# A softmax-attention and S4-convolution kernel: zero matmuls ahead of the first projections, wide gate matmuls, U and H in half-size transfers, norms in pairs, a later set deadline, 71 VectorE sets

## The chip, the cores and the metric

One core of a Trainium2 chip. The metric is the device time of one execution in microseconds (us). The engines are TensorE (PE, with its weight loads shown as PEld), VectorE (DVE), ScalarE (ACT), GpSimd (POOL) and SyncE (SP), whose queue issues nearly all DMAs. Each engine runs its own instructions in their order and waits on semaphores for the others.

## The reference

```python
def reference(A_x, A_wqkv, A_wo, B_u, ..., gate_w):      # x: (1, 2048, 512), u is x
    x = A_x
    g = sigmoid((x * gate_w).sum(-1, keepdims=True))
    a = attention(x, wqkv, wo)          # 32 heads of 16, softmax over all 2048 keys
    b = s4(x, A, B, C, log_dt, Dskip)   # y = causal_conv(x, K) + x * Dskip, per channel
    return g * a + (1 - g) * b
# K[d, l] = Re sum_n C[d,n] exp(dt A[d,n] l) dt B[d,n], l < 2048, n < 128
```

Inputs and output are bf16; scores, sums and the convolution's accumulators are fp32.

## The kernel before

**Attention.** 32 blocks (8 head pairs times 4 stretches of 512 queries) of 16 key tiles are worked as 512 "quads" of four 128x512 score tiles: 2048 tiles in all, three to a group, 683 groups. For group g, `qk(g)` puts three score tiles on PE into one of two PSUM score banks (`SC0`, `SC1`), `ex(g)` takes their exponential on ACT into slots of the ring `ET` (`NS` = 15 slots of 512), and `pv` multiplies a quad with the values into the PSUM bank `OA`. Zero matmuls (`wm`, in `zero` and `qk`) fill PE where its work is thin.

**Sets.** Exponentials are the largest work of ACT, so `decide` gives some tiles to DVE: a set is 12 tiles in four consecutive groups, whose third tiles are computed on DVE (`bits`, four conversions to the bits of a power of two, then `batch`: two masks and a product, into `DZ` and `DU`). In these groups ACT has 128x1024 in place of 128x1536. `WIN` lists the windows of groups in which sets are allowed, their buffers, the least distance and how much idle time DVE must have gathered. The last quad of a block (`kt == 15`, in `pvq`) waited until the set belonging to the block had been multiplied.

**Norms.** After a block, `norm_a` transposes `OA` out of PSUM, `norm_b` divides by the row sums (one reciprocal, one product), and for each second block `norm_c` transposes the pair into `OnT`.

**Convolution.** `bases`, `tables`, `zpart` and `kstage` build K on DVE and PE and write it to DRAM (`gm_kd`); `xrows` writes shifted copies of x (`gm_xs`). `ystage` multiplies: 32 double passes of four quarters, each quarter reading a Toeplitz block `H` (256 KB, five buffers) and a strip `U` (542 KB per double pass, two buffers), loaded by `yloads`. The result, times 1 - g, goes through `Yst` and DRAM into `Yl`.

**Gate and output.** `gate` computes x times gate_w as 64 matmuls with one moving column, then the sigmoid. `outs` multiplies the attention by Wo, and one DVE operation per 128 rows gives g times it plus `Yl`.

**The order.** Nothing is ordered at run time: a planner (`Sched`, `Prog`) with costs per operation (`c`), DMA landing (`lat`), DMA bandwidth (`b`, and `pace` for transfers that keep distance) and priorities writes one instruction order per engine when the kernel is built. A changed cost therefore moves instructions on all engines. The start is by hand: loads on ACT's and SP's queues, nine zero matmuls, transposes of x, then Q and K projections, and the first scores.

Of the kernel before, what the change touches and what calls it, by code (L numbers as in the profile page):

```python
# [304 lines left out]
class Sched:  # L305
# [140 lines left out]
def declare(nc, es):  # L446
# [20 lines left out]
    sb("OT", 512, FP32)  # L467
# [10 lines left out]
    sb("gwT", 4)  # L478
# [53 lines left out]
    B["gd"] = Buf("gd", "dr", P * 16, FP32)  # L532
    B["gd"].t = nc.dram_tensor("gm_gd", [P, 16], FP32)
# [94 lines left out]
def record(nc, p, B, ins):  # L628
# [177 lines left out]
    def seat():  # L806
        while 3 * len(held) + 3 <= len(tiles) or len(tiles) == NSL and len(held) < NG:
            g = len(held)
            n = 2 if g in vec else len(slots(g))
            if plan["at"] + n > NS:  # L810
                plan["at"] = 0
# [3 lines left out]
            plan["at"] = (held[g] + n) % NS  # L815

    def pvq(q, prev, wait):
# [3 lines left out]
        if kt == 15 and wait:  # L821
            yield ("AFTER", wait)
# [7 lines left out]
        sch.open(b if kt < 15 else None)  # L830

# [37 lines left out]

    def ex(g):  # L870
# [3 lines left out]
        op("ACT", lambda a: a.activation(ET(512 * e, [[1, 512 * n]]), sc(0, [[1, 512 * n]]), AF.Exp, scale=DH ** -0.5),  # L874
           [(sc, i, g) for i in range(n)], [(ET, e + i, ts[i]) for i in range(n)] + [(B["tk"], g)], c=.055 + .4267 * n, lat=.105)
# [25 lines left out]
    def batch(i):  # L901
# [3 lines left out]
        def mask(t, a, o, W):  # L905
# [5 lines left out]
        yield ("DVE", dv(2048, 2))  # L911
        op("DVE", lambda v: v.tensor_tensor(u(0, [[1, 2048]]), z(0, [[1, 2048]]), u(0, [[1, 2048]]), ALU.mult),  # L912
           R + [(u, 0, ("m", i))], [(u, 0, i)], c=dv(2048, 2))
# [5 lines left out]
        for t in (u, z):  # L919
            yield ("PE", QUAD)  # L920
            for k, j in enumerate(sets[i]["js"]):
                pv_mm(4 * q + j, t, 512 * k, [(u, 0, i) if t is u else (z, k, (i, k, "t"))], QUAD if k == 0 else 0)
        sch.mark(f"dvp{i}")

    def norm_a(b):
        op("DVE", lambda v: v.transpose(OT(0, [[1, 512]]), OA(0, [[1, 512]])), [(OA, 0, b)], [(OT, 0, b)], c=.64)  # L926

    def norm_b(b):
        w = b % 2
        op("DVE", lambda v: v.reciprocal(Rz(16 * w, [[1, 16]]), OT(16, [[32, 16]])), [(OT, 0, b)], [(Rz, w)], c=.25)  # L930
        op("DVE", lambda v: v.tensor_tensor(ON(16 * w, [[32, 16], [1, 16]]), OT(0, [[32, 16], [1, 16]]),
                                            Rz(16 * w, [[1, 16], [0, 16]]), ALU.mult), [(OT, 0, b), (Rz, w)], [(ON, w)], c=.35)
# [183 lines left out]

    def tables():
        H5 = dv(512, 2)
        yield ("AFTER", "DL80")
# [44 lines left out]
    def kstage(blk):  # L1164
# [3 lines left out]
        Tm = B[f"T{blk % NT}"]  # L1168
# [41 lines left out]
    def xrows():  # L1210
# [8 lines left out]
        for q4 in range(4):  # L1219
            for s0 in range(0, T, 4):  # L1220
# [3 lines left out]
                    [(xP, (0, q4))] + [(xP, (1, s1)) for s1 in range(s0, s0 + 4)], [(xs, (q4, s0))], c=.7, lat=4, b=.86, pace=True)  # L1224
# [4 lines left out]
    UL = 8 * UW - R8 // 2  # L1229

    def yloads():
        yield ("AFTER", YGO)
        for v in range(2 * NBLK):
# [4 lines left out]
            for i in range(2):  # L1238
                yield ("SP", .7)
                dma("SP", lambda e, v=v, U=U, i=i: e.dma_start(U(UL * i, [[1, UL + i]]), xs.dram(v * 16 * UW + R8 - 1 + UL * i, [[D * UW, T], [-1, R8], [1, UL + i]])),  # L1240
                    [(xs, (v // 8, s0)) for s0 in range(0, T, 4)], [(U, i, v)], c=.7, lat=3.5, b=.72, pace=True)
            for q in range(4):
                u = 4 * v + q
                H = B[f"H{u % NHB}"]
                if u >= NHB:
                    yield ("AFTER", f"yh{u - NHB}")
                yield ("AFTER", f"kd{v // 2}")
                yield ("SP", .6)
                dma("SP", lambda e, u=u, H=H: e.dma_start(H(0, [[1, T * HW]]), kd.dram(u * HR * HW + (33 - T) * HW, [[HW, T], [T * HW, R8], [1, T * HW]])),
                    [(kd, (u // 8, u // 2 % 4))], [(H, 0, u)], c=.6, lat=3.5, b=.68, pace=True)  # L1250
# [336 lines left out]
```

## Time and profile before

| | us |
|---|---|
| median of 3 runs | 857.8 (856.04 to 859.12) |
| profiled execution, whole | 860.27 |
| its span | 858.2 |
| first exponential starts | 13.54 |
| last DVE transpose after the exponentials starts | 849.19 |
| mean granted TensorE clock | 0.952 |

A row of instruction groups reads: source line, engine, operation, output <- input with partitions x elements, count | busy us, mean ns of one | idle us just before, and what ended it. Source line L643 is the one line that issues every matmul, so groups are told apart by their tiles. A row of stretches reads: start:end, length, busy us (and count) of PE, PEld, DVE, ACT, POOL, then the granted PE clock (1.00 is full), the share of the DMA engines and GB/s. In the list of instructions in order of time, the first two numbers are start and duration, and the bracket is the idle time before it and its releaser.

### The profile page before, as it was taken

Reading aid. Unit: us, or ns where it says so; the run is one execution under the profiler, and the core shown is the slowest. Engines: PE = TensorE matmul, PEld = TensorE weight load, DVE = VectorE, ACT = ScalarE, POOL = GpSimd, SP = SyncE. Lnnn points to the kernel's source line nnn. Section 1 sums busy time; section 2 is a strip of 40 time slices with the busy share of each in tenths; the row PEclk is TensorE's granted clock in tenths of the full one; section 3 lists DMA queues with packets and bytes.
Section 4 is the critical chain, followed back from the end, with each engine's and each line's share of the span. In section 5 each row is a group of like instructions: output and inputs, shape, how many; then the busy total and the mean of one; then the engine's idle time right before and its main releaser. Section 6 shows DMA issues by size and latency. Waiting matters only on the chain.

```text
span 858.2 us, 35245 instructions
## 1 busy us (share of the span) xinstructions
PE 716.2 (83%) x16105; PEld 317.2 (37%) x16105; DVE 732.2 (85%) x1233; ACT 819.8 (96%) x692; POOL 10.0 (1%) x15
## 2 busy tenths in 40 slices
PE   7879878888887888798888878888887888889884
PEld 3232234342244444354444434444442443322221
DVE  6999896599988979877979786998969889989972
ACT  6999999999988999999999999999999999999895
POOL 4000000000000000000000000000000000000000
PEclk7996899999989999989999999999999999999988
DMA  9464002124576665555445665445566754100000
GB/s 202 81 105 45 12 1 43 26 44 157 152 179 154 162 190 144 142 129 128 111 126 141 177 160 151 98 116 144 119 175 109 204 153 118 19 27 27 28 1 26
DMA packets 154310, 92.71 MB, mean 108 GB/s; under 512 B 116017, under 2 KB 124594, under 8 KB 153778
## 3 DMA queue, kind: packets, MB, share of 16 engines
q1 hardware_dynamic: 152434, 89.55, 42.9%
q8 instruction: 126, 2.06, 1.0%
q10 hardware_dynamic: 1728, 0.92, 0.5%
q14 instruction: 22, 0.18, 0.1%
HBM read 64.46 MB, written 17.31 MB: 95 GB/s over the span
## 4 chain that ended last, share of the span: by engine, by line
ACT 75%; PE 15%; DVE 6%; issue 2%; DMA 1%; ACTq 0%; DVEq 0%
ACT ET L874 75%; PE SC L643 6%; PE MB L643 5%; PE OA L643 4%; DVE DZ L895 2%; DVE fo L1367 1%; DVE DU L912 1%; DMA Wq<-in_A_wqkv_dram 1%; DVE DU L906 0%; DVE Yst L1281 0%; DVE OT L926 0%; DVE DZ L906 0%; ACTq L647 0%; DVE OnT L936 0%; DVE Kt L1190 0%
## 5 line engine op out<-in xcount | busy, mean ns | idle before, releaser
L874 ACT ACTIVATE ET<-SC 128x1536 bf16<-128x1536 f32 (+1 forms) x683 | 813.0, 1460 | 24.3 <-PE SC L643 19.2
L643 PE MATMUL SC<-Qm,KT 32*128 32x512 bf16 x2048 | 288.8, 398 | 110.3 <-ACT ET L874 91.4
L895 DVE TENSOR_SCALAR DZ<-SC 128x512 uint16<-128x512 f32 x268 | 179.6, 685 | 44.0 <-PE SC L643 42.7
L643 PE MATMUL OA<-ET,VE 128*32 128x512 bf16 x1780 | 183.1, 403 | 2.3 <-issue 1.2
L643 PEld LDWEIGHTS SC<-Qm,KT 32*128 32x128 bf16 x2048 | 71.9, 91 | 284.7 <-ACT ET L874 229.2
L643 PE MATMUL OA<-wm 128*32 128x256 bf16 (+3 forms) x845 | 170.3, 364 | 1.2 <-DVE wm L695 1.2
L643 PE MATMUL MB<-U,H 128*16 128x96 bf16 (+15 forms) x8192 | 130.4, 200 | 9.4 <-issue 8.5
L643 PEld LDWEIGHTS MB<-U,H 128*16 128x16 bf16 x8192 | 115.2, 109 | 55.1 <-issue 37.2
L643 PEld LDWEIGHTS OA<-ET,VE 128*32 128x32 bf16 x1780 | 45.9, 94 | 105.1 <-issue 100.1
L912 DVE TENSOR_TENSOR DU<-DZ,DU 128x2048 bf16<-128x2048 bf16 x67 | 82.2, 1227 | 0.5
L940 DVE TENSOR_TENSOR T<-B,DL 128x512 bf16<-128x512 bf16 x192 | 68.8, 415 | 0.0
L643 PEld LDWEIGHTS MB<-T,Z 128*32 128x32 bf16 x2048 | 51.7, 177 | 10.3 <-issue 8.3
L643 PE MATMUL MB<-T,Z 128*32 128x64 bf16 (+1 forms) x2048 | 52.9, 246 | 1.5 <-issue 0.7
L643 PEld LDWEIGHTS OA<-wm 128*32 128x32 bf16 (+2 forms) x845 | 44.1, 97 | 10.4 <-issue 9.1
L906 DVE TENSOR_SCALAR DU<-DZ 128x2048 uint16<-128x2048 uint16 x67 | 46.3, 692 | 0.4
L906 DVE TENSOR_SCALAR DZ<-DZ 128x2048 uint16<-128x2048 uint16 x67 | 45.8, 684 | 0.3
L926 DVE STREAM_TRANSPOSE OT<-OA 128x512 f32<-128x512 f32 x32 | 22.9, 715 | 17.9 <-PE OA L643 17.4
L1281 DVE TENSOR_TENSOR Yst<-MB,gt 128x512 bf16<-128x512 f32 x32 | 21.9, 685 | 16.6 <-PE MB L643 16.3
L940 DVE TENSOR_TENSOR ft<-FP,L 128x1024 f32<-128x1024 f32 (+1 forms) x32 | 34.5, 1113 | 0.5
L643 PE MATMUL OA<-DZ,VE 128*32 128x512 bf16 x268 | 28.0, 402 | 1.9 <-issue 1.1
L643 PE MATMUL OA<-DU,VE 128*32 128x512 bf16 x268 | 27.7, 400 | 0.0
L1190 DVE STREAM_TRANSPOSE Kt<-MB 128x512 f32<-128x512 f32 x16 | 11.4, 712 | 14.5 <-PE MB L643 14.3
(123 smaller groups left out, 435.3 us busy)
## 6 DMA issues: line engine op xcount, KB each, us to landing
H<-gm_kd SPq DMA_DIRECT2D x128, 256.0 KB, 4.0
U<-gm_xs SPq DMA_DIRECT2D x32, 271.2 KB, 4.1
U<-gm_xs SPq DMA_DIRECT2D x32, 271.0 KB, 3.5
T<-B SPq DMA_DIRECT2D x32, 128.0 KB, 3.4
gm_bd<-B16s SPq DMA_DIRECT2D x3, 1024.0 KB, 4.7
B<-gm_bd SPq DMA_DIRECT2D x12, 256.0 KB, 4.0
gm_kd<-Ks SPq DMA_DIRECT2D x64, 40.0 KB, 3.1
gm_xs<-xP SPq DMA_DIRECT2D x16, 136.0 KB, 6.4
```

Source lines behind the costliest of these rows:

```text
L643: op("PE", lambda t: t.matmul(out(), lhsT(), rhs(), start=start, stop=stop, skip_group_check=True, **kw), R, W, c=c, lat=.15, a=a, cfg=cfg)
L874: op("ACT", lambda a: a.activation(ET(512 * e, [[1, 512 * n]]), sc(0, [[1, 512 * n]]), AF.Exp, scale=DH ** -0.5), [(sc, i, g) for i in ran ...
L895: op("DVE", lambda v: v.tensor_scalar(z.u16(512 * k, [[1, 512]]), sc(1024, [[1, 512]]), XS, XB, ALU.mult, ALU.add), [(sc, 2, g)], [(z, k, ...
L906: op("DVE", lambda v: v.tensor_scalar(t.u16(0, [[1, 2048]]), z.u16(0, [[1, 2048]]), a, o, ALU.bitwise_and, ALU.bitwise_or), R, W, c=.07 + ...
L912: op("DVE", lambda v: v.tensor_tensor(u(0, [[1, 2048]]), z(0, [[1, 2048]]), u(0, [[1, 2048]]), ALU.mult), R + [(u, 0, ("m", i))], [(u, 0, ...
L926: op("DVE", lambda v: v.transpose(OT(0, [[1, 512]]), OA(0, [[1, 512]])), [(OA, 0, b)], [(OT, 0, b)], c=.64)
L940: op(eng, lambda v: v.tensor_tensor(o(), a(), b_(), f), R, W, c=c)
L1190: op("DVE", lambda v: v.transpose(Kt(0, [[1, 512]]), MB(0, [[1, 512]])), ky, [(Kt, 0, blk)], c=.66)
L1281: op("DVE", lambda v, w=w, h=h: v.tensor_tensor(Yst(1024 * w + 64 * h, [[16, 4], [128, R8], [1, 16]]), MB(0, [[NC, 4], [1, R8], [R8, 16]]) ...
L1367: op("DVE", lambda v, lt=lt, o=o, off=off: v.scalar_tensor_tensor(o(off, [[1, D]]), MB(0, [[1, D]]), B["g"](lt, [[1, 1]]), Yl(lt, [[16, D] ...
```

## The change

- **Start.** `WARM` = 6 zero matmuls of 512 columns stand between the transposes of x and the first Q projection; on ACT's DMA queue `Wq` is fetched ahead of `Wk`.
- **Gate.** x becomes the moving operand: for each of four 128-row parts of x, four matmuls of 512 columns go to the four column groups of the array at once. Sixteen matmuls replace 64. The sums lie on one partition per column group, so they go through DRAM (`gld`) to become 128x16: four DMAs out, one back, ahead of the sigmoid.
- **Loads.** U comes in four transfers instead of two, H in two instead of one; their planned bandwidth cost is raised (U 1.44 to 2.04 in total, H 0.68 to 0.95), and that of other paced transfers too.
- **Norms.** `norm_b` works on two blocks at once; `OT` is doubled.
- **Set deadline.** A block's last quad no longer waits for its set; the norm of the block waits for both (`whole`, the flag `ob`).
- **Ring.** From group 214 the ring has 21 slots (14 in `ET`, 7 in `EX`), ahead of that 14.
- **Sets.** Windows open at group 190 in place of 210, with another threshold: 71 sets instead of 67.
- **Yst and Yl.** Four channels lie together in both: the output rows read runs of four elements. `Qs` is halved.

```diff
-NS = 15
+NS = 14
+NS2 = 21
+NSG = 214
-WIN = ((210, 400, 3, 5, 1.2), (400, 560, 5, 5, .9), (560, 668, 5, 5, .4))
+WIN = ((190,400,3,5,.9),(400,560,5,5,.9),(560,668,5,5,.6))
+UN4 = 4
+HN = 2
+UB = 1.02
+HB = .95
+WARM = 6
...
+load_w("Wq", 0, 0, P, 0)
 load_w("Wk", D, 0, P, 0)
-load_w("Wq", 0, 0, P, 0)
...
+    for k in range(WARM):
+        mm(lambda: OA(0, [[1, 512]]), lambda: wm(0, [[1, 128]]), lambda: wm(0, [[1, 512]]), [(wm, 0)], [(OA, 0, "warm")])
     for q4 in range(4):
         proj_mm("Q", 0, 0, oa, q4)
...
+    def whole(b):
+        if b in last and (last[b] is None or last[b] in sch.flag) and f"pv{16 * b + 15}" in sch.flag:
+            sch.mark(f"ob{b}")
 def pvq(q, prev, wait):
-        if kt == 15 and wait:
-            yield ("AFTER", wait)
...
+        if kt == 15:
+            last[b] = wait
+            sch.do(lambda: whole(b))
...
-            for i in range(2):
+            for i in range(UN4):
                 yield ("SP", .7)
...
+                for i in range(HN):
+                    yield ("SP", .6)
+                    n = T * HW // HN
+                    dma("SP", lambda e, u=u, H=H, i=i, n=n: e.dma_start(H(n * i, [[1, n]]), kd.dram(u * HR * HW + (33 - T) * HW + n * i, [[HW, T], [T * HW, R8], [1, n]])),
+                        [(kd, (u // 8, u // 2 % 4))], [(H, i, u)], c=.6, lat=3.5, b=HB / HN, pace=True)
...
-            op("DVE", lambda v, w=w, h=h: v.tensor_tensor(Yst(1024 * w + 64 * h, [[16, 4], [128, R8], [1, 16]]), MB(0, [[NC, 4], [1, R8], [R8, 16]]),
-                                                B["gt"](0, [[0, 4], [16, R8], [1, 16]]), ALU.mult),
+            op("DVE", lambda v, w=w, h=h: v.tensor_tensor(Yst(1024 * w + 64 * h, [[128, R8], [4, 16], [1, 4]]), MB(0, [[1, R8], [R8, 16], [NC, 4]]),
+                                                B["gt"](0, [[16, R8], [1, 16], [0, 4]]), ALU.mult),
...
-        for lt in range(16):
-            for q4 in range(4):
-                mm(lambda lt=lt: MB(lt, [[1, 1]]), lambda lt=lt, q4=q4: xT(q4 * S + 128 * lt, [[1, 128]]), lambda q4=q4: gwT(q4, [[1, 1]]),
+        for q4 in range(4):
+            yield ("PE", MM)
+            for c in range(4):
+                mm(lambda c=c: MB(0, [[1, 512]], 32 * c, 32), lambda q4=q4: gwT(32 * q4, [[1, 32]]),
+                   lambda c=c, q4=q4: xT(q4 * S + 32 * c, [[1, 32], [P, 16]]),
...
-                                                                            Yl(lt, [[16, D]]), ALU.mult, ALU.add),
+                                                                            Yl(4 * lt, [[64, D // 4], [1, 4]]), ALU.mult, ALU.add),
...
 def norms():
-            yield ("AFTER", f"pv{16 * b + 15}")
+            yield ("AFTER", f"ob{b}")
...
+                yield ("DVE", .9, 1)
+                norm_b(b, 2)
```

What the planner makes of it, at three places. First ACT, from the gate's exponential (`ge<-gp`) to the first sets; `ET<-SC` is a group's exponential, 1024 wide where DVE takes a tile. Before:

```order
L874 ACTIVATE ET<-SC 128x1536 x54
L1317 ACTIVATE ge<-gp 128x16
L874 ACTIVATE ET<-SC 128x1536 x158
L874 ACTIVATE ET<-SC 128x1024 x4
L874 ACTIVATE ET<-SC 128x1536
```

and now:

```order
L907 ACTIVATE ET<-SC 128x1536 x50
L1368 ACTIVATE ge<-gp 128x16
L907 ACTIVATE ET<-SC 128x1536 x141
L907 ACTIVATE ET<-SC 128x1024 x4
L907 ACTIVATE ET<-SC 128x1536
```

The first set moves from group 213 to group 192, and four sets stand before the group at which the first one stood; the gate's exponential comes four groups earlier. Over the whole program 285 groups have 1024 instead of 269; the later sets are spread differently, with 30 of them from group 400 to 600 in place of 32.

Second PE, at the gate, some 43 groups into the program (`SC<-Qm,KT` scores, `OA<-ET,VE` values, `wm` zeros). Before:

```order
L643 MATMUL SC<-Qm,KT 128x512 x2
L643 MATMUL MB<-gwT,xT 128x1 x8
L643 MATMUL OA<-wm 32x512 x4
L643 MATMUL OA<-wm 32x256 x4
L643 MATMUL SC<-Qm,KT 128x512 x3
L643 MATMUL OA<-ET,VE 32x512 x4
```

and now:

```order
L661 MATMUL SC<-Qm,KT 128x512 x2
L661 MATMUL MB<-xT,gwT 32x512 x16
L661 MATMUL SC<-Qm,KT 128x512 x3
L661 MATMUL OA<-ET,VE 32x512 x4
L661 MATMUL SC<-Qm,KT 128x512
```

Before, eight pieces of eight narrow matmuls stood in 12 successive groups, each beside zero matmuls; now one piece of sixteen wide ones stands in one group, without zeros.

Third SP's queue, at the first U and H loads of the convolution (`Qm<-gm_qd` are the queries of the next block, `T<-B` a table of the K stage). Before:

```order
L1240 DMA U_166<-gm_xs 128x1x1084
L1240 DMA U_166<-gm_xs 128x1x1085
L1249 DMA H_168<-gm_kd 128x1x1024
L1249 DMA H_169<-gm_kd 128x1x1024
L1249 DMA H_170<-gm_kd 128x1x1024
L1249 DMA H_171<-gm_kd 128x1x1024
```

and now:

```order
L1284 DMA U_168<-gm_xs 128x1x544 x3
L1284 DMA U_168<-gm_xs 128x1x537
L1295 DMA H_170<-gm_kd 128x1x512
L770 DMA Qm<-gm_qd 16x512 x4
L1295 DMA H_170<-gm_kd 128x1x512
L1295 DMA H_171<-gm_kd 128x1x512 x2
```

Each load of before is two now, and other DMAs (here the queries of a block) stand between the halves. Over the program U has 128 issues in place of 64 and H 256 in place of 128.

More of the change, by code (lines that the diff above doesn't have):

```diff
@@ L54 @@
 NT = 1
+TB = 5
 NZ = 1
@@ L331, in mark, with do @@
             self.flag.add(name)
+    def do(self, f):
+        if self.p.cap is not None:
+            self.p.cap.append(f)
+        else:
+            f()
     def open(self, b):
@@ L476, in declare @@
     sb("hpi", 1, FP32)
-    sb("gwT", 4)
+    sb("gwT", 128)
+    sb("gl", 512, FP32)
     sb("wm", D)
@@ L667, in record @@
     op("POOL", lambda g: g.memset(B["Dr"](0, [[1, D]]), 0.0), [], [(B["Dr"], 0)], c=.4)
+    op("POOL", lambda g: g.memset(B["gwT"](0, [[1, 128]]), 0.0), [], [(B["gwT"], 1)], c=.1)
     op("POOL", lambda g: g.memset(B["sel"](0, [[1, 32]]), 0.0), [], [(B["sel"], 0)], c=.1)
@@ L868, in qk, with et @@
                 zero(zbank(), 512, (32 * jz, 0), 32, 128, 0, 128, "R")
+    def et(i):
+        return (ET, 512 * i) if i < NS else (B["EX"], 512 * (i - NS))
     def ex(g):
@@ L888, in pv @@
         for k, s in enumerate(own):
-            pv_mm(s, ET, 512 * home[s], [(ET, home[x], x) for x in (own if k == 0 else [s])], QUAD if k == 0 else 0)
+            pv_mm(s, *et(home[s]), [(et(home[x])[0], home[x], x) for x in (own if k == 0 else [s])], QUAD if k == 0 else 0)
     def bits(g):
@@ L910, in batch @@
         mask(u, 0x007F, 0x3F00, [(u, 0, ("m", i))])
-        yield ("DVE", dv(2048, 2))
-        op("DVE", lambda v: v.tensor_tensor(u(0, [[1, 2048]]), z(0, [[1, 2048]]), u(0, [[1, 2048]]), ALU.mult),
-           R + [(u, 0, ("m", i))], [(u, 0, i)], c=dv(2048, 2))
+        for h in range(MH):
+            n = 2048 // MH
+            yield ("DVE", dv(n, 2))
+            op("DVE", lambda v, h=h, n=n: v.tensor_tensor(u(n * h, [[1, n]]), z(n * h, [[1, n]]), u(n * h, [[1, n]]), ALU.mult),
+               R + [(u, 0, ("m", i))], [(u, 1 + h, i)], c=dv(n, 2))
         yield ("DVE", .6)
@@ L1115, in bases, with tbuf @@
                 sch.mark(f"bw{qr}{k}")
+    def tbuf(blk):
+        return 0 if blk < TB else blk % NT
     def tables():
@@ L1223, in xrows @@
                                                               xP((q4 * T + s0) * XW + 16 - PAD, [[XW, 4], [1, UW]])),
-                    [(xP, (0, q4))] + [(xP, (1, s1)) for s1 in range(s0, s0 + 4)], [(xs, (q4, s0))], c=.7, lat=4, b=.86, pace=True)
+                    [(xP, (0, q4))] + [(xP, (1, s1)) for s1 in range(s0, s0 + 4)], [(xs, (q4, s0))], c=.7, lat=4, b=1.1, pace=True)
             sch.mark(f"xs{q4}")
@@ L1276, in ystage @@
                            lambda q=q, j=j, n=n, U=U: U((4 * j + q) * UW + 1, [[1, n]]),
-                           [(H, 0, hu)] + [(U, i, u) for i in range(2)], ky, q + m == 0, m == NM - 1, pos=(0, 32 * j), c=c if j == 0 else 0,
+                           [(H, i, hu) for i in range(HN)] + [(U, i, u) for i in range(UN4)], ky, q + m == 0, m == NM - 1, pos=(0, 32 * j), c=c if j == 0 else 0,
                            a=n // 8, cfg="C")
```

99 lines of the change are left out of this document (57 added, 42 removed).

## The prediction

> **What bounds the kernel now.** I read the page's busy shares first, then the chain that ended last, then ScalarE's (ACT's) instruction groups with shapes kept apart, and last a table of stretches, because a share over 858 us says nothing of the stage in which it arises.
>
> ```profile
> span 858.2 us, 35245 instructions
> PE 716.2 (83%) x16105; PEld 317.2 (37%) x16105; DVE 732.2 (85%) x1233; ACT 819.8 (96%) x692; POOL 10.0 (1%) x15
> ACT 75%; PE 15%; DVE 6%; issue 2%; DMA 1%; ACTq 0%; DVEq 0%
> L874 ACT ACTIVATE ET<-SC 128x1536 bf16<-128x1536 f32 x414 | 577.3, 1667 | 18.6 <-PE SC L643 14.4 <-PE OA L643 3.2
> L874 ACT ACTIVATE ET<-SC 128x1024 bf16<-128x1024 f32 x269 | 263.5, 1140 | 5.7 <-PE SC L643 4.8 <-PE OA L643 0.8
> 13.54 1.45 ACT L874 ACTIVATE ET<-SC 128x1536 bf16<-128x1536 f32 x1 [2.74 <-PE SC L643]
> ```
>
> ACT is busy 96% and holds 75% of the chain. It does one thing: 683 exponentials, 414 of three score tiles and 269 of two (the third tile of such a group goes to VectorE, DVE). So the span is a head of 13.5 us, 683 exponentials end to end, the gaps between them (18.6 + 5.7 less the head's 2.74 = 21.6 us) and a tail. Only four things can shorten it: fewer tiles on ACT, fewer gaps, a shorter head, a shorter tail. The gaps by stretch are the stretch's length less its ACT column:
>
> ```profile
> core 0: us, PE busy (x) PEld busy (x) DVE busy (x) ACT busy (x) POOL busy (x), PEclk, DMA share, GB/s
> 75.00:95.00 20.00, 19.91 (x194) 5.43 (x191) 15.92 (x29) 18.18 (x15) 0.00 (x0) 0.55 0.01 2
> 235.00:300.00 65.00, 52.27 (x1634) 28.95 (x1631) 57.11 (x115) 60.04 (x44) 0.00 (x0) 0.92 0.65 166
> 300.00:400.00 100.00, 85.97 (x2618) 44.21 (x2617) 87.83 (x148) 97.24 (x85) 0.00 (x0) 0.95 0.57 149
> 400.00:480.00 80.00, 69.33 (x2111) 36.56 (x2104) 65.36 (x115) 79.48 (x72) 0.00 (x0) 1.00 0.52 131
> 480.00:570.00 90.00, 74.82 (x2371) 38.10 (x2370) 77.56 (x131) 86.66 (x78) 0.00 (x0) 1.00 0.57 144
> 750.00:815.00 65.00, 57.42 (x453) 14.96 (x449) 60.71 (x86) 58.04 (x55) 0.00 (x0) 0.91 0.09 28
> ```
>
> The gate (75 to 95) loses 1.8 us; the convolution from 235 to 570 loses 5.0 + 2.8 + 0.5 + 3.3 = 11.6; the output stage (750 to 815) loses 7.0. Together these are 20.4 of the 21.6.
>
> **Sets: 67 to 71.** Each set takes four tiles from ACT, so 16 more tiles leave it; in the order 285 groups have two tiles instead of 269. A tile is worth 577.3/414 - 263.5/269 = 1.394 - 0.980 = 0.415 us (busy time, so overlaps are out). 16 x 0.415 = **-6.7 us**. That is whole as long as DVE takes the tiles in time. A set costs DVE four conversions, two masks and a product:
>
> ```profile
> L895 DVE TENSOR_SCALAR DZ<-SC 128x512 uint16<-128x512 f32 x268 | 179.6, 685 | 44.0 <-PE SC L643 42.7
> L912 DVE TENSOR_TENSOR DU<-DZ,DU 128x2048 bf16<-128x2048 bf16 x67 | 82.2, 1227 | 0.5
> L906 DVE TENSOR_SCALAR DU<-DZ 128x2048 uint16<-128x2048 uint16 x67 | 46.3, 692 | 0.4
> L931 DVE TENSOR_TENSOR ON<-OT,Rz 128x256 bf16<-128x256 f32 x32 | 13.7, 427 | 1.1
> L930 DVE RECIPROCAL Rz<-OT 128x16 f32<-128x16 f32 x32 | 7.6, 238 | 0.0
> L1367 DVE SCALAR_TENSOR_TENSOR fo<-MB,g,Yl 128x512 bf16<-128x512 f32 x12 | 13.5, 1127 | 1.3 <-PE MB L643 1.2
> L1549 DVE SCALAR_TENSOR_TENSOR fo<-SC,g,fp 128x512 bf16<-128x512 f32 x3 | 2.1, 740 | 0.0
> L1281 DVE TENSOR_TENSOR Yst<-MB,gt 128x512 bf16<-128x512 f32 x32 | 21.9, 685 | 16.6 <-PE MB L643 16.3
> ```
>
> (179.6 + 82.2 + 2 x 46.3)/67 = 5.3 us (the second mask is of the first's form), so four sets add 21.2 us to DVE. Against that, 15 pairs of norms become one reciprocal and one product each: twice 0.67 becomes about 0.25 + 0.70 (a 512-element operation has 0.69 in these rows), -0.38 x 15 = -5.7. DVE ends near 732 + 21 - 6 - 6 (the output stage, below) = 741 us, 88% of a span of 844: busier, but not the bound. The four sets stand before group 212, where the old order had none, that is in the stretch 235 to 300 with 65 - 57.1 = 7.9 us of DVE free; later sets move apart, so the surplus spreads. I take the whole -6.7.
>
> **Gate.** 64 matmuls of one column are replaced by 16 of 512 columns in four column groups, at once.
>
> ```profile
> 70.17 0.35 PE L643 MATMUL MB<-gwT,xT 128*128 128x1 bf16 x8
> 84.00:86.00 2.00, 2.00 (x23) 0.50 0.00 0
> 92.10 0.62 PE L643 MATMUL OA<-ET,VE 128*32 128x512 bf16 x4
> 93.88 0.40 PE L643 MATMUL OA<-ET,VE 128*32 128x512 bf16 x4
> ```
>
> The second row is a stretch of PE alone: busy 2.00 us, granted clock 0.50; it reads so in every stretch from 74 to 92 us. Four value matmuls take 0.62 us, against 0.40 once it is back. ACT then waits for PE now and then: the 1.8 us. Sixteen wide matmuls in four concurrent columns take about 4 x 0.22 = 0.9 us of PE in one group, and without the low clock the waits go: **-1.8 us** (0 if something else lowers the clock). The sum through DRAM adds five DMAs and one wait of an ACT exponential on the last; in the order it stands 8 groups (some 11 us) behind the matmuls, and two landings fit in that, even at the 3.4 us of a 128 KB transfer (below). Nothing reads the gate before the convolution.
>
> The Trainium skill (TensorE: Matmul & The Clock Gate, part 1) says that about 3.4 us of sustained matmul activity opens the gate again. The rows above disagree: PE is busy 2.00 of 2.00 us at 0.50, and stayed so for 20 us. By the page the low clock would end by itself and this term would shrink to some 0.5 us; by the row it ends with the narrow matmuls.
>
> **Head.** Six zero matmuls go behind the transposes, and the Q weights are fetched ahead of the K weights.
>
> ```profile
> Wk<-in_A_wqkv_dram ACTq DMA_DIRECT2D x1, 128.0 KB, 5.6
> 2.22 0.60 ACTq L647 DMA_DIRECT2D Wq<-in_A_wqkv_dram  x1
> 5.11 0.84 PE L643 MATMUL SC<-idb,x0n 128*128 128x128 bf16 x12 [0.31 <-DMA x0n<-in_A_x_dram]
> 8.50 1.89 PE L643 MATMUL OA<-xT,Wq 128*128 128x512 bf16 x4 [2.32 <-DMA Wq<-in_A_wqkv_dram]
> 9.52 1.28 ACT L874 ACT_TABLE_LOAD   x1
> 10.18 1.91 PE L643 MATMUL SC<-xT,Wk 128*128 128x512 bf16 x4
> 759.71 1.04 PE L643 MATMUL MB<-Wo,OnR 128*128 128x512 bf16 x4
> 8.00:9.00 1.00, 0.50 (x2) 0.50 1.07 317
> ```
>
> The last row is of the table of stretches for PE alone: busy, then granted clock. PE idles 2.3 us and its clock falls, so eight projections cost 1.89 + 1.91 us; at full clock four cost 1.04. The weight that stands a place earlier in the queue is issued about 0.5 us before the 2.22 of this one and lands 5.6 us later, at some 7.3 us; the other then lands at about 8.5. If the zeros hold the clock, they end at 6.2 + 6 x 0.22 = 7.5, Q is done at 8.5, K at 9.5 in place of 12.1, and the first exponential, whose table is loaded by 10.8, starts near 11.1: -2.4. If the clock falls all the same, the zeros take 2.5 us, Q starts at 8.7, and it is +0.2. The twelve transposes at 0.84 us are already at the full pace, so I take **-2.0**.
>
> **U and H in halves.** 192 more DMAs on SP's queue, the same bytes.
>
> ```profile
> 238.62 2.28 SPq L1249 DMA_DIRECT2D H<-gm_kd  x1
> 241.00 0.50 PE L643 MATMUL MB<-U,H 128*16 128x104 bf16 x15 [2.31 <-issue]
> 242.09 1.45 ACT L874 ACTIVATE ET<-SC 128x1536 bf16<-128x1536 f32 x1 [1.97 <-PE SC L643]
> H<-gm_kd SPq DMA_DIRECT2D x128, 256.0 KB, 4.0
> T<-B SPq DMA_DIRECT2D x32, 128.0 KB, 3.4
> SPq L286 <- PE MB L643: 156.9, 72, 11.4
> ```
>
> Here PE stops for 2.3 us in the middle of one accumulation, at a matmul that waits for no data, and ACT's gap of 1.97 follows. The chain above counts 2% of the span as such "issue" time; I read the stops as instruction fetches that queue behind a large transfer issued just before. A transfer of half the size in front should halve the queue. Bounds: 0 (the bytes in flight are the same) to -11.6 (all of that stretch's gaps). I take **-3**, a quarter. SP itself has room: it waits 156.9 us for PE.
>
> The Trainium skill (SBUF — State Buffer, the DMA setup-cost knee) speaks against this edit: some 2 us per transfer whatever its size, so coalesce. The rows agree in kind (3.4 us for 128 KB, 4.0 for 256). By the rule alone the term would be a loss; since loads already overlap here (below), I give it to a rival.
>
> **Output stage.** The Yst layout now keeps four channels together, so the output rows read Yl in runs of four instead of one element in 16. The same operation takes 1127 ns with Yl and 740 with a contiguous operand; 16 x 0.39 = 6.2 us of DVE, in a stage where DVE is busy 60.7 of 65 us and ACT loses 7.0: PE waits there until DVE has emptied a score bank. Bounds 0 to -7.0; one more set falls into the same groups (+5.3), so **-3**. Yst's own read of PSUM gets a step of 512 B instead of 32: its 685 ns are already those of the contiguous read of a score tile (685), so I cost it at nothing.
>
> **Later set deadline, ring of 21 tiles.**
>
> ```profile
> 801.21 1.45 ACT L874 ACTIVATE ET<-SC 128x1536 bf16<-128x1536 f32 x1 [1.54 <-PE OA L643]
> ```
>
> These let ACT run further ahead of PE's value matmuls. ACT's direct waits for those are the 3.2 + 0.8 = 4.0 us in its rows; this one, the longest, lies in the output stage and is counted there. The rest I set against the new: a longer queue on SP ahead of the Q-mask loads, and a busier DVE. Together **+2** (from -2 to +8).
>
> Sum: -6.7 - 1.8 - 2.0 - 3 - 3 + 2 = **-14.5 us**. The profiled execution took 860.27 us (2.1 around its span), which is 2.5 above the median of the runs, 857.8; the difference goes on the median: **843.3 us**.
>
> **Rivals.** (1) Only the sure terms hold (-6.7 - 1.8 - 2.0 + 2 = -8.5): fetch stops and the output stage stay as they are, 849.3. For it: half-size transfers leave as many bytes in flight. (2) All gaps go: -6.7 - 1.8 - 2.4 - 11.6 - 7.0 = -29.5, 828.3. Against: the clock falls in the output stage too. (3) The change doesn't do what it says: DVE is late with the moved sets, PE waits for the score bank, and the 6.7 come back as gaps, with no stop won: -1.8 - 2.0, 854. For it: 7.9 us free against 21. (4) Slower: the loads bound the convolution. Its 128 passes run from 234 to 740 us, 3.95 us each; H and half of two U loads in series would be 4.0 + 1.9 = 5.9 us before, so they overlap; as twice 3.4 plus 3.4 it would be 10.2. It decides once loads arrive at more than 3.95 us a pass; each 0.2 us above costs 26 us, 843.3 + 26 = 869. Against it: SP's 157 us of waiting for PE.
>
> **How the numbers follow.** Forecast 0.47 (838 to 848), rival 1 0.24, rival 2 0.11, rival 3 0.12, rival 4 0.06. The range 833 to 854 leaves out rival 4, half of 2 and some of 3. A measurement tells 0.3%, 2.6 us, from no change: faster 0.89, same 0.05 (part of rival 3), slower 0.06.
>
> **What would show it.** Two-tile exponentials 285; clock at 1.0 from 70 to 95 us; first exponential near 11 us, Q projections at 1.04 us for four; "issue" under 1.5% of the chain; fo at some 740 ns and ACT's gaps from 735 to 800 us halved. Wrong it would be if ACT's gaps stay above 18 us, or if PE waits for U or H by name.

## The result, and the profile after

| | before | after |
|---|---|---|
| median of 4 runs each, us | 856.92 (849.18 to 859.12) | 830.70 (830.42 to 832.74) |
| ratio | | 0.9715, 95% interval 0.9651 to 0.9778 |
| profiled execution, whole, us | 860.27 | 830.66 |
| its span, us | 858.2 | 828.7 |
| mean granted TensorE clock | 0.952 | 0.990 |

The change is faster, as forecast, but by 26 us here, not 14.5. Timed again beside the experiments, the kernel before took 841.6 to 858.5 us in 79 further executions, those marked slow left out, with a median of 852.2. Against that the gain is 21.5 us.

The page after, its busy shares and chain, then ScalarE's (ACT's) and VectorE's (DVE's) groups with shapes kept apart:

```profile
span 828.7 us, 35337 instructions
PE 686.8 (83%) x15986; PEld 311.3 (38%) x16013; DVE 743.4 (90%) x1231; ACT 808.6 (98%) x692; POOL 10.2 (1%) x16
ACT 91%; DVE 4%; PE 3%; DMA 1%; issue 0%; ACTq 0%; DVEq 0%
L907 ACT ACTIVATE ET<-SC 128x1536 bf16<-128x1536 f32 x334 | 470.0, 1738 | 1.7 <-PE SC L661 1.7
L907 ACT ACTIVATE ET<-SC 128x1024 bf16<-128x1024 f32 x196 | 201.0, 1198 | 1.7 <-PE SC L661 1.6
L907 ACT ACTIVATE EX<-SC 128x1536 bf16<-128x1536 f32 x64 | 98.4, 1610 | 2.1 <-PE SC L661 1.9
L907 ACT ACTIVATE EX<-SC 128x1024 bf16<-128x1024 f32 x89 | 93.6, 1198 | 0.0
L1418 DVE SCALAR_TENSOR_TENSOR fo<-MB,g,Yl 128x512 bf16<-128x512 f32 x12 | 8.9, 740 | 1.8 <-PE SC L661 1.8
```

ACT now holds 91% of the chain in place of 75%, and 285 exponentials have two tiles. Their gaps are 1.7 + 1.7 + 2.1 = 5.5 us in place of 21.6 (24.3 with the head's 2.74). None ends with a value matmul (`OA`); in the kernel before 4.0 us did. The means of one (1738 against 1667 ns) rise because an exponential that finds its scores ready starts while the last one still runs.

Stretches, with the columns of the table before; the last row is the output stage, which now lies 25 us earlier:

```profile
75.00:95.00 20.00, 15.41 (x142) 4.80 (x140) 19.37 (x32) 20.00 (x17) 0.00 (x0) 1.00 0.05 10
235.00:300.00 65.00, 55.33 (x1738) 30.45 (x1738) 62.83 (x108) 65.00 (x55) 0.00 (x0) 1.00 0.60 154
300.00:400.00 100.00, 86.04 (x2640) 42.18 (x2632) 92.20 (x151) 100.00 (x91) 0.00 (x0) 1.00 0.54 140
400.00:480.00 80.00, 69.97 (x2084) 38.21 (x2083) 69.55 (x128) 79.46 (x71) 0.00 (x0) 0.98 0.56 141
480.00:570.00 90.00, 77.98 (x2415) 40.17 (x2415) 82.05 (x141) 88.22 (x78) 0.00 (x0) 0.96 0.53 131
725.00:790.00 65.00, 54.60 (x590) 16.58 (x596) 63.18 (x94) 63.51 (x62) 0.00 (x0) 1.00 0.09 24
```

From 235 to 400 us ACT never stops (it lost 7.8 there), and from 235 to 570 it loses 2.3 us in place of 11.6. The output stage loses 1.5 in place of 7.0, at full clock. At the gate the clock is full too, yet the gate brought a wait of its own just ahead of that stretch, in the list of instructions:

```profile
11.59 1.45 ACT L907 ACTIVATE ET<-SC 128x1536 bf16<-128x1536 f32 x1
67.66 3.60 PE L661 MATMUL MB<-xT,gwT 128*32 128x512 bf16 x16
71.63 4.14 ACT L907 ACTIVATE ET<-SC 128x1536 bf16<-128x1536 f32 x3 [1.66 <-PE SC L661]
```

The sixteen wide gate matmuls take 3.60 us, not 0.9, and ACT waits 1.66 us behind them.

**A finer measure.** Gaps miss what an exponential loses when it overlaps the one ahead of it. In every trace the ends of two neighbouring exponentials lie 1.343 us apart (median) where the later one has three tiles and 0.917 where it has two; all above that I call loss. The span is then: start of the first exponential, plus 683 such steps (802.7 us with 269 two-tile groups, 795.9 with 285), plus loss, plus the tail behind the last exponential. From one profiled execution of each kernel, loss split at groups 110 and 600:

| kernel | first exp. | loss to g110 | g110 to g600 | from g600 | tail | median us |
|---|---|---|---|---|---|---|
| before | 13.54 | 4.4 | 19.3 | 8.7 | 9.55 | 856.9, later 852.2 |
| b_yl | 13.09 | 1.1 | 16.4 | 1.6 | 9.97 | 846.7 |
| b_split | 11.35 | 1.1 | 7.8 | 7.9 | 9.69 | 844.3 |
| after | 11.59 | 2.9 | 6.8 | 2.0 | 9.38 | 830.7 |
| after2 | 11.23 | 2.9 | 7.8 | 2.0 | 9.39 | 831.6 |
| a_gate2 | 11.17 | 1.1 | 5.2 | 2.0 | 9.38 | 827.7 |
| a_yl | 11.01 | 3.0 | 5.5 | 9.4 | 9.17 | 837.2 |
| a_merge | 11.38 | 3.1 | 7.4 | 2.0 | 9.61 | 833.5 |
| a_warm | 12.64 | 2.9 | 6.3 | 3.2 | 9.38 | 831.3 |
| a_ring | 11.17 | 3.0 | 9.8 | 6.8 | 9.38 | 837.8 |
| a_rep2 | 11.34 | 3.1 | 7.7 | 3.7 | 23.27 | 844.6 |
| b_rep1 | 12.10 | 3.3 | 19.9 | 1.8 | 39.65 | 879.3 |

Each row is one execution, so a loss of some us can belong to the execution and not to the kernel. Between the first row and "after": head -1.95, tiles -6.8, loss 32.4 to 11.8 = -20.6, tail -0.2; together the 29.5 us between the two spans.

### The profile page after: what moved, and what is told of

It reads as the page before. It is cut to its first block, busy times and chain, and to the rows that moved or that the text cites. A ratio compares the mean times of both kernels' runs of the same rounds, so it can differ in the third digit from the quotient of the medians.

```text
span 828.7 us, 35337 instructions
## 1 busy us (share of the span) xinstructions
PE 686.8 (83%) x15986; PEld 311.3 (38%) x16013; DVE 743.4 (90%) x1231; ACT 808.6 (98%) x692; POOL 10.2 (1%) x16
## 4 chain that ended last, share of the span: by engine, by line
ACT 91%; DVE 4%; PE 3%; DMA 1%; issue 0%; ACTq 0%; DVEq 0%
ACT ET L907 71%; ACT EX L907 19%; DVE DZ L928 2%; PE SC L661 1%; PE MB L661 1%; PE OA L661 1%; DVE DU L947 1%; DMA ldt<-in_B_log_dt_dram 1%; DVE fo L1418 0%; DVE DU L939 0%; DVE OT L963 0%; DVE DZ L939 0%; ACT L907 0%; ACT L1508 0%; ACTq L623 0%
## 5 line engine op out<-in xcount | busy, mean ns | idle before, releaser
L907 ACT ACTIVATE ET<-SC 128x1536 bf16<-128x1536 f32 (+1 forms) x530 | 648.9, 1538 | 3.4 <-PE SC L661 3.3
L661 PE MATMUL SC<-Qm,KT 32*128 32x512 bf16 x2048 | 277.6, 386 | 122.8 <-ACT ET L907 85.9
L928 DVE TENSOR_SCALAR DZ<-SC 128x512 uint16<-128x512 f32 x284 | 189.7, 685 | 35.2 <-PE SC L661 33.7
L907 ACT ACTIVATE EX<-SC 128x1024 bf16<-128x1024 f32 (+1 forms) x153 | 184.3, 1370 | 2.1 <-PE SC L661 1.9
L661 PE MATMUL OA<-ET,VE 128*32 128x512 bf16 x1394 | 154.2, 392 | 1.4 <-ACT ET L907 0.9
L661 PE MATMUL OA<-wm 128*32 128x256 bf16 (+3 forms) x773 | 153.9, 354 | 1.2 <-DVE wm L714 1.2
L661 PE MATMUL MB<-U,H 128*16 128x72 bf16 (+15 forms) x8192 | 128.1, 198 | 2.3 <-issue 2.2
L947 DVE TENSOR_TENSOR DU<-DZ,DU 128x2048 bf16<-128x2048 bf16 x71 | 87.3, 1233 | 0.8
L661 PEld LDWEIGHTS OA<-ET,VE 128*32 128x32 bf16 x1394 | 39.2, 93 | 77.3 <-issue 72.9
L661 PE MATMUL OA<-EX,VE 128*32 128x512 bf16 x370 | 55.6, 394 | 0.1
```

Of the source, the lines that this page charges most:

```text
L661: op("PE", lambda t: t.matmul(out(), lhsT(), rhs(), start=start, stop=stop, skip_group_check=True, **kw), R, W, c=c, lat=.15, a=a, cfg=cfg)
L907: op("ACT", lambda a: a.activation(E(at, [[1, 512 * n]]), sc(0, [[1, 512 * n]]), AF.Exp, scale=DH ** -0.5), [(sc, i, g) for i in range(n)] ...
L928: op("DVE", lambda v: v.tensor_scalar(z.u16(512 * k, [[1, 512]]), sc(1024, [[1, 512]]), XS, XB, ALU.mult, ALU.add), [(sc, 2, g)], [(z, k, ...
L947: op("DVE", lambda v, h=h, n=n: v.tensor_tensor(u(n * h, [[1, n]]), z(n * h, [[1, n]]), u(n * h, [[1, n]]), ALU.mult), R + [(u, 0, ("m", i ...
```

## The experiments

Names with a_ are the changed kernel with one thing undone or altered, names with b_ the kernel before with one thing added. The question at first was whether transfer size, load pacing, or the slack of ring and deadline removes the loss. Most of these kernels compare less than they seem to, because the planner writes a new order for each. They are therefore sorted by that: **order held** means that PE, DVE and ACT run the same instructions in the same order as the kernel compared with, but for the instructions that the change itself takes out. Not all were timed on one chip; beside them, the kernel before has medians from 850.7 to 853.7 us by chip, so a difference of 3 us between kernels timed on different chips says nothing.

### Order held

**a_yl, b_yl: the Yst layout alone.**

```diff
-Yst(1024 * w + 64 * h, [[128, R8], [4, 16], [1, 4]]) ... Yl(4 * lt, [[64, D // 4], [1, 4]])
+Yst(1024 * w + 64 * h, [[16, 4], [128, R8], [1, 16]]) ... Yl(lt, [[16, D]])      (a_yl; b_yl the reverse)
```

> The changed kernel with the old Yst layout, so that the output rows read Yl with one element in 16. The output operation goes back from 740 to 1127 ns. If VectorE's time in the output stage made the 7.0 us of gaps there, they return whole and the time is 836 us; by the prediction's term half of them, 833.5 us; if it was the clock or the ring, 831 us.

> The kernel before with only the new Yst layout. Output operation 740 ns. If the parts add, the gain is some 6 us, all of it after 735 us: 845.5 against 851.5 us. By the prediction's term 3 us: 848.5. By theory 'together' under 2 us.

Measured: a_yl 837.22 us (833.87 to 839.23), 6.5 above the changed kernel, on another chip; b_yl 846.67 us, ratio 0.9934 (0.9893 to 0.9974) to the kernel before, -5.8 us. The group of the output operation in a_yl and in b_yl, then the output stage of a_yl and that of after2 (the changed kernel timed again) in the tables of stretches:

```profile
L1418 DVE SCALAR_TENSOR_TENSOR fo<-MB,g,Yl 128x512 bf16<-128x512 f32 x12 | 13.5, 1128 | 2.8 <-PE MB L661 2.8
L1367 DVE SCALAR_TENSOR_TENSOR fo<-MB,g,Yl 128x512 bf16<-128x512 f32 x12 | 8.9, 740 | 0.3 <-PE MB L643 0.3
```

```profile
725.00:800.00 75.00, 63.71 (x593) 16.99 (x590) 67.42 (x95) 67.60 (x64) 0.00 (x0) 0.91 0.08 22
```

```profile
725.00:800.00 75.00, 62.88 (x653) 18.80 (x660) 69.96 (x106) 73.50 (x71) 0.00 (x0) 1.00 0.09 24
```

With the old layout ACT loses 7.4 us of 75, with the new 1.5, and the clock falls to 0.91 with it. Both directions give the same 6 to 7 us, and in the table above the loss from group 600 on moves by 7.4 and 7.1 us with the layout; what else differs between the rows of before and b_yl is not the layout's doing. So in these two orders nearly all of the output stage's gaps came from DVE's slow read of Yl. Another order can lose there for other reasons: a_win and a_ring, below, have the new layout and lose 10.5 and 6.8 us from group 600 on.

**b_split, a_merge: the transfer size alone.** Only the U and H transfers are split in two or joined, after the planner has done its work; pacing as it was in each kernel.

```diff
 for f, q, a in log:                 # what the planner has written, now emitted
+    if hasattr(a[1], "part"):       # b_split: two pieces in place of one
+        for fn, W in a[1].part:
+            prog.dma(a[0], fn, a[2], W)
+        continue
...
+    if part is not None:            # a_merge: the first piece brings both, the second goes
+        if part[0]:
+            continue
+        a = (a[0], a[1], a[2], part[1])
```

> The kernel before with its order on PE, VectorE and ScalarE kept, but every U and H transfer issued as two of half the size, one behind the other. Theory 'transfer size': the longest PE stop falls from 1.8 to 2.3 us to about 1 us, the granted clock rises from 0.97 to 0.98 or more, 846 us or less against 852. Theory 'order': within 2 us of before.

> The changed kernel with its order on PE, VectorE and ScalarE kept, but the halves of H and the quarters of U issued as one transfer of twice the size at the place of the first piece. Theory 'transfer size': stops of over 1.5 us return, granted clock falls below 0.985, 835 us or more. Theory 'order' (undoing the halves cost 7 us because the planner then wrote another order): within 2 us of the changed kernel on this chip.

Measured: b_split 844.28 us (840.64 to 849.11), ratio 0.9917 (0.9888 to 0.9947), against 851.6 for the kernel before beside it: -7.3 us. a_merge 833.45 us (831.69 to 836.98), against 831.56 (828.63 to 833.22) for after2 on the same chip: 1.9 more, with overlapping ranges. The convolution in the tables of stretches, in the kernel before and in b_split:

```profile
235.00:590.00 355.00, 299.61 (x9281) 156.55 (x9277) 306.08 (x539) 343.42 (x293) 0.00 (x0) 0.97 0.57 145
```

```profile
235.00:590.00 355.00, 302.81 (x9588) 161.21 (x9584) 314.37 (x553) 352.32 (x304) 0.00 (x0) 1.00 0.57 148
```

The DMA share is the same 0.57, so the bytes in flight are too; ACT runs 352.3 of 355 us in place of 343.4, and the clock is 1.00. PE's waits of the kind "issue" (total us, times, longest us), in before, b_split, a_merge and the changed kernel:

```profile
PE MB L643 <- issue: 9.2, 12, 2.3
PE SC L643 <- issue: 3.6, 4, 1.9
PE OA L643 <- issue: 2.4, 2, 1.2
```

```profile
PE MB L647 <- issue: 8.1, 24, 2.2
PE OA L647 <- issue: 0.7, 1, 0.7
PE SC L647 <- issue: 0.3, 1, 0.3
```

```profile
PE MB L666 <- issue: 8.1, 25, 1.0
PE SC L666 <- issue: 0.8, 2, 0.4
PE OA L666 <- issue: 0.2, 1, 0.2
```

```profile
PE MB L661 <- issue: 4.8, 21, 0.8
```

In the old order the stops do not vanish. They fall from 15.2 to 9.1 us and come as more and shorter pieces: 15.2/18 = 0.84 us on average before, 9.1/26 = 0.35 in b_split. The longest is still 2.2 us, against the 1 us that was expected, but stops over 1 us are rare now: seven with 11.0 us together in the trace of before, five with 7.3 in that of b_yl (the same order with whole transfers), one in b_split. The time at half clock between groups 110 and 600 falls with them, from 23.9 and 20.5 us to nothing. That a short stop costs little because ACT still has a filled score bank is likely and not shown by a run.

What the stops are can be read from the traces. The page of before has a queue of instruction packets:

```profile
q8 instruction: 126, 2.06, 1.0%
```

That is one packet of 16 KB for each 256 or so of PE's 32,000 instructions. Counted in PE's own matmuls, weight loads and semaphore instructions, all eleven stops over 0.4 us in before lie 193 to 195 instructions behind a multiple of 256, and one of these packets lands 1.3 to 1.7 us ahead of the end of each. The twelve such stops of b_yl and the six of b_split keep to one place among 256 in the same way. So they are instruction fetches, as the prediction read them. That a fetch queues behind the large transfer ahead of it fits b_split; no trace shows the queue itself. The split also gives PE 137 more semaphore instructions (251 in place of 114), which moves the places in its work where a block ends; that this had no part in the gain is not shown.

In the changed kernel's order the size decides little. With full-size transfers a_merge has the stops back (9.1 us in place of 4.8), but only one reaches 1.0 us, and its loss from group 110 to 600 is 7.4 us against 6.8 and 7.8. So something besides the halves keeps the loss down there: the wider pacing, the ring, the later deadline, the other norms or simply the order. The pacing alone decides little either (a_pace below, in nearly the same order). No run has this order with full-size transfers and the old pacing together, so which of them it is stays open.

The Trainium skill (SBUF — State Buffer, the DMA setup-cost knee) would have DMA-bound transfers coalesced into the largest single one. b_split, at a DMA share of 0.57 and bound by ACT, shows smaller transfers paying.

**a_gate2: the gate's moving columns.**

```diff
-xT(q4 * S + 32 * c, [[1, 32], [P, 16]])      # neighbouring columns 256 B apart
+xT(q4 * S + 32 * c, [[P, 16], [1, 32]])      # runs of 32 neighbours
-v.tensor_copy(gl(0, [[1, 512]]), MB(0, [[1, 512]]))
+v.tensor_copy(gl(0, [[16, 32], [1, 16]]), MB(0, [[1, 32], [32, 16]]))
```

> The changed kernel with the gate's 512 moving columns read as 16 runs of 32 neighbours instead of single columns 256 B apart; the copy out of PSUM puts them in the old order. If the stride of the moving operand made the four matmuls 3.60 us, they take some 0.9 us, ScalarE's gap of 1.66 us at 70 us goes, 829 us. If their length comes from something else (the wait on the last V copy, the column groups), it stays at 3.6 us and 830.7 us.

Measured: 827.73 us (826.75 to 830.25). The gate in the list of instructions:

```profile
62.25 15.36 ACT L907 ACTIVATE ET<-SC 128x1536 bf16<-128x1536 f32 x11
67.25 1.05 PE L661 MATMUL MB<-xT,gwT 128*32 128x512 bf16 x16
68.56 0.68 DVE L1360 COPY gl<-MB 128x512 f32<-128x512 f32 x1
```

1.05 us in place of 3.60, eleven exponentials without a gap, and the permuted copy out of PSUM takes 0.68 us, as the plain one does. The stride was the cause. In the table this saves 1.8 us up to group 110. The median is the lowest of all, 3 to 4 us below the changed kernel's, but on a chip on which the kernel before was 3 us faster too than beside after2 (850.7 against 853.7): more than the 1.8 us is not shown.

**a_warm: no zero matmuls in the head** (`WARM = 0`).

> The changed kernel without the six zero matmuls, Q weights still first, the same order otherwise. If the zeros hold the clock: the clock falls at 7 to 11 us, the first exponential starts at 13 us instead of 11.0 to 11.6, and the time is 1 to 2 us longer. If the order of the two weights was enough: 11.0 to 11.6 us and no change.

Measured: 831.28 us (830.10 to 832.47), against 831.56 for after2 on the same chip. In its trace the clock did fall (0.79 from 5 to 13 us, 1.00 in after2) and four Q projections took long:

```profile
7.90 1.89 PE L661 MATMUL OA<-xT,Wq 128*128 128x512 bf16 x4 [1.77 <-DMA Wq<-in_A_wqkv_dram]
12.64 1.45 ACT L907 ACTIVATE ET<-SC 128x1536 bf16<-128x1536 f32 x1 [1.34 <-PE SC L661]
```

In this one execution the first exponential starts 1.4 us later than in after2, as was expected without the zeros, but the times show no difference. Nor does the old head always lose: b_split has it, and its clock held (1.00 from 5 to 13 us), its first exponential at 11.35.

### Order written anew

**a_rep2, b_rep1: a new order.** One planner constant moves, the gap that it leaves for instruction fetches. It is not the order alone that moves: b_rep1 has some 110 zero matmuls more, and a_rep2 one set more, 289 two-tile groups in place of 285.

```diff
-FETCH = 3.4
+FETCH = 3.5
```

> The changed kernel, planned anew with one constant of the planner (its gap between instruction fetches) 3.5 instead of 3.4; no transfer, tile or instruction count is meant to change. Theory 'order': the time moves by 3 to 10 us, most likely upwards. Theories on the parts: within 2 us.

> The kernel before, planned anew with the planner's gap between instruction fetches 3.5 instead of 3.4. Theory 'order': the time moves by 2 to 8 us either way. Theories on the parts: within 2 us.

Measured: a_rep2 844.63 us (841.29 to 845.06), 13 above after2; b_rep1 879.33 us (877.14 to 881.58), ratio 1.0336 (1.0283 to 1.0389). The chain of b_rep1 behind its last exponentials:

```profile
818.99 18.63 ACT ET L874 x15
837.67 0.39 PE SC L643 x2
838.06 0.98 PE MB L643 x4
839.13 1.14 DVE fo L1367
840.32 1.05 PE MB L643 x4
841.46 1.14 DVE fo L1367
...
869.54 1.13 DVE fp L1367
870.67 0.64 DVE OT L926
```

The output rows, which the other order puts beside exponentials, come after them, one PE product and one DVE operation at a time: the tail is 39.65 us in place of 9.55. In a_rep2 it is 23.27 in place of 9.39. A new order thus moves the time by more than any part of the change measured with the order held. It also means that the following runs can't give the worth of their parts.

**a_halves, a_pace, b_halves, b_halfpace: halves and pacing.** The b_ kernels take over the split loops of the change, with the old and with the new pacing.

```diff
-UN4 = 4, HN = 2                                        +UN4 = 2, HN = 1                           (a_halves)
-UB = 1.02, HB = .95, others b=.95 and b=1.1            +UB = .72, HB = .68, others b=.7 and .86   (a_pace)
+UN4 = 4, HN = 2, UB = .72, HB = .68                                                               (b_halves)
+UN4 = 4, HN = 2, UB = 1.02, HB = .95, others b=.95 and b=1.1                                      (b_halfpace)
```

> The changed kernel with U in two transfers and H in one again, its slower load pacing kept. Theory 'transfer size' (PE's fetch stops queue behind large transfers): the stops come back, PE's MB issue idle from 4.8 to some 9 us with single stops over 2 us, ScalarE's gaps from 5.5 to some 15 us, 840 us. Theory 'pacing' (what matters is how far apart the loads are issued): gaps stay under 8 us, 831 to 833 us. Theory 'slack' (the longer ring and later deadline absorb stops that still happen): stops return to 9 us but the gaps stay under 8 us, 831 to 833 us.

> The changed kernel with the load pacing of before (U 0.72, H 0.68, others 0.70 and 0.86 us) and the half-size transfers kept. Theory 'transfer size': no change, 831 us, gaps under 8 us. Theory 'pacing': stops return, gaps some 15 us, 840 us. Theory 'slack': no change beyond 2 us.

> The kernel before with only the half-size U and H transfers, its pacing, ring, deadline and sets as they were. Theory 'transfer size': the longest PE stop falls from 2.3 to about 1.2 us, the gaps from 235 to 570 us from 11.6 to some 4 us, 849 against 857 us. Theories 'pacing' and 'slack': within 2 us of before.

> The kernel before with the half-size transfers and the slower pacing together, nothing else. Theories 'transfer size' and 'pacing': the gaps from 235 to 570 us fall from 11.6 to some 3 us, 848 us. Theory 'slack': stops under 1 us, but the gaps fall by less than 4 us, 854 us or more.

Measured: a_halves 837.89 us, of which 3.0 are a longer tail (12.38); a_pace 833.86 us (828.96 to 837.62), its order on ACT the same and on PE nearly; b_halves 851.55, ratio 1.0012 (0.9977 to 1.0047); b_halfpace 852.54, ratio 1.0019 (0.9981 to 1.0058). Read alone, the last two would say that the halves are worth nothing. With the order held they are worth 7.3 us. In b_halves the trace shows what took back at least part of it, a wait of PE for a late H, which neither before nor b_split has:

```profile
PE MB L647 <- DMA H<-gm_kd: 5.3, 1, 5.3
```

ACT stops for 5.3 us behind it. b_halfpace, with the wider pacing, has no such wait, and its loss from group 110 to 600 is 13.0 us, against 17.8 in b_halves and 7.8 in b_split.

**a_ring, b_ring, a_dead, a_win, b_ringylh: ring, deadline, sets.** b_ring has the ring of the change alone, b_ringylh ring, Yst layout and halves. a_win has 273 two-tile groups, so 12 tiles are back on ACT; b_ringylh and b_halfpace have 273 too, one set more than the kernel before.

```diff
-NS = 14, NS2 = 21, NSG = 214                                       +NS = 15, NS2 = 15, NSG = 999   (a_ring; b_ring the reverse)
+        if kt == 15 and wait: yield ("AFTER", wait)                                                (a_dead)
-WIN = ((190,400,3,5,.9),(400,560,5,5,.9),(560,668,5,5,.6))
+WIN = ((210, 400, 3, 5, 1.2), (400, 560, 5, 5, .9), (560, 668, 5, 5, .4))                          (a_win)
```

> The changed kernel with a ring of 15 score tiles throughout instead of 14 and then 21. Theory 'slack': ScalarE waits for PE's value matmuls again, the gaps after group 214 grow by some 6 us, 837 us. Theory 'transfer size': the ring is worth nothing, 830 to 832 us.

> The kernel before with only the ring of 14 and then 21 score tiles. Undoing the ring in the changed kernel cost 7 us. If the parts add, the gain here is 6 to 7 us: 845 against 851.5 us. If the ring only pays where the stops are short (theory 'together'), it is worth under 2 us here, as the halves were.

> The changed kernel with the old deadline: the last value tile of a block waits for the block's set again. Theory 'slack': gaps grow by 3 us or more, 834 us or more. Theory 'transfer size': 830 to 832 us.

> The changed kernel with the 67 sets of before. By the prediction's term the 16 tiles go back to ScalarE at 0.42 us each: 830.7 + 6.7 = 837.4 us, gaps as they are (10 to 12 us over the full pace). If DVE was late with the added sets, part of it comes back as smaller gaps: 834 us.

> The kernel before with the ring, the new Yst layout and the half-size transfers, old sets, gate, head, norms and pacing. Additive by the undone parts (7 + 6.5 + 7): some 831 + 6.7 for the sets + 2 to 3 for gate and head, 838 to 841 us. If the halves are worth nothing whatever stands around them: 839 + 5 = 844 to 846 us.

Measured: a_ring 837.80 us; b_ring 852.55, ratio 1.0023 (0.9995 to 1.0051); a_dead 830.00; a_win 844.62; b_ringylh 847.65, ratio 0.9947 (0.9917 to 0.9977). ACT's waits in a_ring:

```profile
ACT ET L907 <- PE SC L661: 6.6, 10, 1.7
ACT ET L907 <- PE OA L661: 6.0, 4, 2.5
```

The 6.0 us of direct waits for value matmuls, zero in the changed kernel, are about the whole loss of that run. Yet the order differs too, and with the long ring b_ring still waits 4.7 us for one and a_win 5.8 us for two. So the ring is a possible cause in a_ring and not a proven one. In a_win the 12 tiles explain 5.1 of the 14 us; the rest is mostly loss from group 600 on (10.5 in place of 2.0). b_ringylh missed both of its forecasts, 838 to 841 and 844 to 846 us; PE waits 4.4 us for a late H in it too. With the old deadline a_dead is no slower, but in an order of its own.

**after2**, the changed kernel again on the chip of a_merge and a_warm.

> The changed kernel again: 830 to 832 us, granted clock 0.981 to 0.990, as in its first four runs.

Measured: 831.56 us (828.63 to 833.22).

## Why the prediction was right in direction and wrong in size

- **What bounds it** held: ACT end to end, and four ways to shorten it. The sets' **-6.7** is in the account as -6.8 for 16 tiles. DVE, at 90%, was not late: from 235 to 300 us, where sets were added, ACT runs 65.00 of 65 us.
- **Output stage, -3: the first step that failed.** The price per operation (1127 to 740 ns) and the bounds (0 to -7.0) were right, the value between them was not. I set half against one more set in these groups. Measured with the order held, the layout is worth 5.8 us in the old order and 6.5 in the new: next to the upper bound.
- **The gaps of the convolution, -3 of 11.6: the second, and the larger.** I took "a quarter" because the bytes in flight stay the same. They do, and yet ACT's gaps from 235 to 570 us fall by 9.3 us. The halves alone are worth 7.3 us in the old order, where they leave one fetch stop over 1 us of seven. In the changed kernel's own order taking them back costs 1.9 us, which the spread of the runs does not tell from nothing. So the sum went wrong in leaving three quarters of these gaps in place; the halves are enough to remove most of them, but the change has something else that is enough too, and what that is stays open. The view that I had not used was the groups' pace: from group 110 to 600 the old order loses 19.3 and 16.5 us in two traces (before, b_yl), the changed kernel 6.8.
- **Later deadline, ring, longer queue, +2: not borne out.** In the trace of the changed kernel no gap of ACT waits for `OA`, and PE waits for no U or H (in after2 once for an H, 1.1 us). What each is worth stays open.
- **Gate, -1.8: wrong on the price, and on what lowers the clock.** 0.9 us became 3.60, and a gap of 1.66 took the place of the 1.8. I had counted columns and not looked at how they lie. The clock stays at 1.00, but I read its fall as the work of the narrow matmuls, and b_yl and b_split, with the same narrow matmuls in the same order, have 1.00 from 70 to 95 us as well and lose 1.1 us up to group 110, the changed kernel 2.9. Here the gate as written is a small loss against a good execution.
- **Head, -2.0** came as -1.95 between the two profiles, but that is luck in part: the old head starts its first exponential at 11.23 to 13.54 us by execution (eight traces), and the 2 us are the price of a bad one.
- **The base.** The sum began from one execution with a mean clock of 0.952 and took two measurements to agree within 0.3%. In the 79 others the clock goes from 0.951 to 0.989, the times lie up to 2% apart, and the span falls by some 3.2 us for each 0.01 (correlation -0.77). So 857.8 was 6 us above the usual. From 852.2 the same sum gives 837.7, which leaves 7 us of the 12.6 to the terms above.

Of the rivals, "all gaps go" (828.3) is nearest, and its two large steps, the convolution and the output stage, are the right ones, though the gate's gap stayed. The layout's -5.8 and the halves' -7.3, measured in the old order, and the tiles' -6.8 make -19.9 of the 21.5 us between 852.2 and 830.7. No run shows that they add up so, and a_merge speaks against reading it as the halves' share in the changed kernel.

## What to carry to other kernels

Where a planner writes the order, first learn what a new order alone does to the time, and then test a part with the order held. Profile more than one execution before summing terms: up to group 110 the same order lost 4.4 us in one trace and 1.1 in two others. Where an engine stops, look at the length of the single stops and not only at their total. And undo a part in the new kernel as well as adding it to the old one: the halves were worth 7.3 us in the old order and some 1.9, within the spread of the runs, in the new.

## What the hardware showed unexpectedly

**The clock falls in windows.** In all 20 traces every stretch at 0.50 inside the span lasts a multiple of 3.41 us. Four such windows of the kernel before, in the table of stretches:

```profile
222.70:226.12 3.42, 2.78 (x22) 0.81 (x22) 3.35 (x6) 3.42 (x4) 0.00 (x0) 1.00 0.11 38
226.12:229.53 3.41, 1.88 (x29) 0.54 (x27) 3.31 (x6) 3.41 (x4) 0.00 (x0) 1.00 0.40 119
229.53:232.94 3.41, 3.39 (x31) 0.63 (x31) 3.31 (x6) 3.41 (x4) 0.00 (x0) 0.50 0.97 268
232.94:236.36 3.42, 2.94 (x118) 1.53 (x110) 3.32 (x7) 3.42 (x4) 0.00 (x0) 1.00 1.05 274
```

PE is busy 1.88 of 3.41 us (0.55) in the second window, and the third runs at half clock. From 20 us to 820 us of the 20 traces, cut into such windows: behind a window at full clock with PE busy under 0.6, 33 of 41 next ones ran at half clock; between 0.6 and 0.7, 26 of 208; between 0.7 and 0.8, 18 of 1436; above, 7 of 2853. So 1.4 us or more of idle time within one window (0.4 of 3.41) was mostly followed by a window at half pace. The Trainium skill (TensorE: Matmul & The Clock Gate, part 1) gives windows of about 3.4 us; the traces agree on the length.

**A moving operand whose columns lie 256 B apart** is slow. The gate's group in the changed kernel, then in a_gate2:

```profile
L661 PE MATMUL MB<-xT,gwT 128*32 128x512 bf16 x16 | 3.6, 1031 | 0.0
```

```profile
L661 PE MATMUL MB<-xT,gwT 128*32 128x512 bf16 x16 | 1.0, 382 | 0.0
```

The same 16 matmuls of 512 columns take 1031 ns each with single columns 256 B apart, and 382 ns with runs of 32 neighbours.
